# Moving the two half chunks of the last group's output behind its other chunks

## The chip, the cores and the metric

The kernel runs on one core of a Trainium2 chip. Its time is the device time of one execution in microseconds (us), and the figure given is the median of several executions. The core has five engines with an instruction stream each: TensorE (PE in the profile), VectorE (DVE), ScalarE (ACT), GpSimd (POOL) and SyncE (SP), which issues most of the transfers here.

## What is computed

A transformer block with adaptive layer norm over a sequence of 2048 rows of 512 bf16 values: a local dilated attention (32 heads of 16, window 8, stride 2), then a gated feed-forward layer with 1792 hidden columns. The reference, cut to the outer frame and the second half:

```python
def _B_ref(x, w_gate, w_up, w_down):
    g = jnp.einsum('bsd,df->bsf', x, w_gate)
    u = jnp.einsum('bsd,df->bsf', x, w_up)
    h = _gelu(g) * u
    return jnp.einsum('bsf,fd->bsd', h, w_down)
...
h = _layernorm(x, axis=-1) * (1 + ca) + sa
x = x + ga * _A_ref(h, A_wqkv, A_wo)
h = _layernorm(x, axis=-1) * (1 + cb) + sb
x = x + gb * _B_ref(h, B_w_gate, B_w_up, B_w_down)
return x
```

The six vectors `sa` to `gb` come from `silu(c) @ w_mod`. Only the last line and the last product, `h` by `w_down`, are touched by the change, and only for the last 512 of the 2048 rows.

## The kernel before

The rows are split into five groups (`GROUPS`): two of 256 rows and three of 512. Each group passes through a layer norm, the products for q, k and v, the attention, a second layer norm, and the feed-forward layer (`emit_ffn`). The kernel first records all of its work as operations (`Plan.op`), numbered in the order in which they are recorded; each has an engine, an estimated time and a function that issues its instructions. `Plan.order` then puts them into the order of the hand-kept list `ORDER`, and `Plan.emit` issues them in that order. Every engine executes its own instructions in the order in which they were issued, so `ORDER` fixes, for each engine separately, what comes after what. Waits between engines follow from the tiles that are read and written and from the buffers of the tile pools.

`emit_ffn` for one group works in two steps. First, for 14 pieces of 128 hidden columns, 4 matmuls with `Wg` and 4 with `Wu` (line 800) fill two accumulators; ScalarE takes the gelu of the one (line 809) and copies the other (line 811); VectorE multiplies them into the tile `hht` (line 812). Second, the output is made in chunks of 128 rows (`c4`): 14 matmuls over the hidden pieces (line 827) add up the accumulator `y_ps`, VectorE adds the residual row `x` to it and writes `ot` (line 840), and SyncE issues the transfer of `ot` to the output (line 843). The 14 matmuls are recorded as four operations, of 4, 4, 4 and 2 matmuls.

The last group has four such chunks. The last chunk is cut into two halves of 256 of the 512 columns (`parts = 2`), each with its own accumulator, its own 14 matmuls of half the width, its own addition and its own transfer. I call the four chunks **c0**, **c1**, **c2** and the two halves **A** (columns 0 to 255) and **B** (columns 256 to 511). Their operations have the numbers:

| part | matmuls (4, 4, 4, 2) | addition | transfer |
|---|---|---|---|
| c0 | 986, 987, 988, 989 | 990 | 991 |
| c1 | 992, 993, 994, 995 | 996 | 997 |
| c2 | 998, 999, 1000, 1001 | 1002 | 1003 |
| A | 1004, 1005, 1006, 1007 | 1008 | 1009 |
| B | 1010, 1011, 1012, 1013 | 1014 | 1015 |

The accumulators come from a pool with 4 buffers (`psF`), which the gate and up products use as well, and `ot` from a pool with 2. A tile takes its buffer at its first use in `ORDER`, and waits there until the tile that had the buffer before is done. The end of `ORDER` before the change reads

```python
949, 950, 986, 980, 992, 993, 994, 998, 987, 988, 995, 996, 997, 1010, 989, 990, 991, 1011, 999, 1004, 1005, 1012,
1006, 1007, 1013, 1008, 1014, 1015, 1000, 1001, 1009, 1002, 1003,
```

so TensorE ends with the last six matmuls of c2 (1000 and 1001), after both halves; VectorE adds c1, c0, A, B, c2, in this order; and SyncE sends c1, c0, B, A, c2.

Of the kernel before, what the change touches and what calls it, by code (L numbers as in the profile page):

```python
# [15 lines left out]
NEG = -1.0e9  # L16

ORDER = [
    55, 5, 0, 7, 8, 9, 42, 43, 40, 41, 2, 6, 13, 33, 34, 44, 45, 137, 139, 16, 275, 138, 140, 10, 46, 141, 35, 36, 37,
    47, 273, 265, 1, 51, 48, 267, 56, 142, 143, 11, 144, 38, 39, 49, 53, 274, 52, 145, 12, 50, 57, 58, 146, 147, 54,  # L20
    59, 148, 150, 60, 266, 62, 268, 276, 277, 269, 149, 61, 278, 280, 270, 14, 66, 271, 64, 28, 159, 279, 272, 67,
    468, 63, 93, 155, 458, 65, 160, 156, 15, 70, 3, 71, 4, 151, 469, 32, 460, 92, 459, 281, 21, 282, 68, 284, 283, 69,
# [35 lines left out]
    941, 961, 963, 943, 962, 942, 944, 945, 964, 916, 918, 965, 917, 956, 958, 919, 920, 921, 922, 924, 923, 915, 903,  # L58
    971, 957, 959, 960, 973, 967, 966, 968, 969, 981, 925, 982, 983, 972, 974, 951, 970, 975, 984, 953, 927, 926, 928,
    929, 930, 985, 952, 954, 955, 937, 939, 932, 931, 933, 946, 936, 934, 938, 940, 935, 948, 977, 979, 976, 978, 947,  # L60
    949, 950, 986, 980, 992, 993, 994, 998, 987, 988, 995, 996, 997, 1010, 989, 990, 991, 1011, 999, 1004, 1005, 1012,
    1006, 1007, 1013, 1008, 1014, 1015, 1000, 1001, 1009, 1002, 1003,
]


# [149 lines left out]
def kernel(  # L215
# [28 lines left out]
    pl = Plan(tc)  # L244
# [24 lines left out]
    def pri(stage, g, step=0.0):  # L269
        base = {"ln1": PRI_LN1[g], "qkv": PRI_QKV[g], "att": 100 * g, "ln2": 100 * g, "ffn": 100 * g + 1000,  # L270
                "glu": 100 * g - 200}[stage]
        return base + step
# [7 lines left out]
    def h_cols(t, g, dt):  # L280
        n = GROUPS[g][1]
        return t[g][:, dt, 0:n] if len(t[g].shape) == 3 else t[g][:, 0:n // P, dt, :]
# [118 lines left out]
    for b in (1, 0):  # L401
        dma(524e3, lambda dq, b=b: dq.dma_start(
            out=wm01[:, :, b * D:(b + 1) * D], in_=w_mod[:, b * D:(b + 1) * D].rearrange("(t p) n -> p t n", p=P)),
            w=[(wm01, b)], pri=-999.5 + 0.5 * (1 - b), bw=340e3)
# [6 lines left out]
    for d4 in range(4):  # L411
# [3 lines left out]
            pri=-987, bw=200e3)  # L415
# [7 lines left out]
    for i in range(2):  # L423
# [3 lines left out]
            w=[(WdP, ft) for ft in range(lo, hi)], pri=-888 + i, bw=335e3, late=1.0)  # L427
# [359 lines left out]
    def emit_ffn(g):  # L787
        n = GROUPS[g][1]
        nf = SG // n
        hh = []  # L790
        for f0 in range(0, FT, nf):
            p = pri("ffn", g, f0)
            gu = []
            for Wt in (Wg, Wu):
                ps = T("psF", [P, nf, n], F32, "g_ps" if Wt is Wg else "u_ps", "ffn")

                def mm(Wt=Wt, ps=ps, f0=f0):
                    for ft in range(f0, f0 + nf):
                        for dt in range(DT):
                            nc.tensor.matmul(ps[:, ft - f0, :], lhsT=Wt[ft // 7][:, dt, ft % 7 * P:(ft % 7 + 1) * P],  # L800
                                             rhs=h_cols(h2, g, dt), start=(dt == 0), stop=(dt == DT - 1))

                pe(0.866, mm, r=[Wt[f0 // 7], Wt[(f0 + nf - 1) // 7], h2[g]], w=[ps], pri=p)
                gu.append(ps)
            gl = T("gl", [P, nf, n], BF16, "gl")
            ub = T("ub", [P, nf, n], BF16, "ub")
            ht = T("hh", [P, nf, n], BF16, "hht")
            p = pri("glu", g, f0)
            act(0.485, lambda gl=gl, ps=gu[0]: nc.scalar.activation(out=gl[:], in_=ps[:], func=ACT.Gelu_apprx_tanh),  # L809
                r=[gu[0]], w=[gl], pri=p, table="gelu")  # L810
            act(0.475, lambda ub=ub, ps=gu[1]: nc.scalar.copy(out=ub[:], in_=ps[:]), r=[gu[1]], w=[ub], pri=p)  # L811
            dve(0.335, lambda gl=gl, ub=ub, ht=ht: nc.vector.tensor_tensor(out=ht[:], in0=gl[:], in1=ub[:],  # L812
                                                                          op=ALU.mult), r=[gl, ub], w=[ht], pri=p)
            hh.append(ht)
        for c4 in range(n // P):
            gc = GROUPS[g][0] // P + c4
            ot = T("ot", [P, D], BF16, "ot")
            parts = 2 if g == NG - 1 and c4 == n // P - 1 else 1
            w = D // parts
            for part in range(parts):  # L820
                y_ps = T("psF", [P, w], F32, "y_ps", "ffn")
                p = pri("ffn", g, 20 + c4)
                c0 = w * part
                for lo, hi in ((0, 4), (4, 8), (8, 12), (12, 14)):
                    def down(lo=lo, hi=hi, c4=c4, y_ps=y_ps, c0=c0, w=w):
                        for ft in range(lo, hi):
                            nc.tensor.matmul(y_ps[:], lhsT=hh[ft // nf][:, ft % nf, c4 * P:(c4 + 1) * P],  # L827
                                             rhs=WdP[:, ft, c0:c0 + w], start=(ft == 0), stop=(ft == FT - 1))

                    pe(0.2165 / parts * (hi - lo), down, r=hh[lo // nf:hi // nf] + [(WdP, ft) for ft in range(lo, hi)],  # L830
                       w=[y_ps], pri=p)
                p = pri("glu", g, 20 + c4)
                if g < PLAIN:
                    dve(0.6, lambda ot=ot, y_ps=y_ps: nc.vector.tensor_tensor(
                        out=ot[:], in0=y_ps[:], in1=gbB[:], op=ALU.mult), r=[y_ps, gbB], w=[(ot, part)], pri=p)
                    dve(0.335, lambda c4=c4, ot=ot: nc.vector.tensor_tensor(
                        out=ot[:], in0=ot[:], in1=x[g, c4], op=ALU.add), r=[(ot, part), x.key(g, c4)], w=[(ot, part)],
                        pri=p)
                else:
                    dve(0.06 + 0.54 / parts, lambda c4=c4, ot=ot, y_ps=y_ps, c0=c0, w=w: nc.vector.tensor_tensor(  # L840
                        out=ot[:, c0:c0 + w], in0=y_ps[:], in1=x[g, c4][:, c0:c0 + w], op=ALU.add),
                        r=[y_ps, x.key(g, c4)], w=[(ot, part)], pri=p)
                dma(131e3 / parts, lambda dq, gc=gc, ot=ot, c0=c0, w=w: dq.dma_start(
                    out=out[0, gc * P:(gc + 1) * P, c0:c0 + w], in_=ot[:, c0:c0 + w]), r=[(ot, part)], pri=p, late=-0.85)
# [4 lines left out]
    for g in range(NG):  # L849
        ln(g, hT[g], 0, pri("ln1", g), "ln1", LN1_TAGS[g])  # L850
        emit_qkv(g)
        if g == 0:
            mod_row(2, gaB, pri("att", 0, 3.5))
            mod_cols(3, 4, pri("att", 0, 3.6), 8)
            mod_row(5, gbB, pri("att", 0, 3.7))
            dve(1.14, lambda: nc.vector.tensor_tensor(out=woP[:], in0=woP[:], in1=_ap(gaB[:], [[0, 4], [1, D]]),
                                                      op=ALU.mult), r=[woP, gaB], w=[woP], pri=pri("att", 0, 4))
        emit_attention(g)
        if g >= 1:
            emit_ffn(g - 1)  # L860
        if g == PLAIN:
            for f0 in range(0, FT, 2):
                dve(0.6, lambda f0=f0: nc.vector.tensor_tensor(
                    out=WdP[:, f0:f0 + 2, :], in0=WdP[:, f0:f0 + 2, :], in1=_ap(gbB[:], [[0, 2], [1, D]]),
                    op=ALU.mult), r=[(WdP, f0), (WdP, f0 + 1), gbB], w=[(WdP, f0), (WdP, f0 + 1)], pri=500)
    emit_ffn(NG - 1)
    for o in pl.ops:
        if o.dma and o.eng == "sp":
# [30 lines left out]
```

## Time and profile before

| | |
|---|---|
| median of 5 executions | 244.95 us |
| the five | 244.67, 244.72, 244.95, 246.33, 246.73 us |
| the profiled execution | 246.33 us |
| its span, first to last instruction | 244.6 us |
| VectorE, ScalarE, GpSimd busy | 163.5 us (67%), 148.4 us (61%), 25.8 us (11%) |

The profiled execution is one of the five. Its span is 1.73 us shorter than its time, which is what lies before the first and after the last instruction. The last stretch of the span, engine by engine (busy time in us):

| stretch, us | PE | DVE | ACT | POOL |
|---|---|---|---|---|
| 228 to 232 | 3.95 | 0.76 | 0.96 | 0 |
| 232 to 236 | 4.00 | 0.70 | 0 | 0 |
| 236 to 240 | 3.95 | 1.43 | 0 | 0 |
| 240 to 244 | 0.73 | 0.70 | 0 | 0 |

The granted TensorE clock is full (1.000) over the whole span. The second step of the last group's feed-forward layer starts at 228.44 us, and from then on TensorE has nothing else to do.

A row of the timeline gives the start, the duration from the first to the last of a merged run of instructions, the engine, the line, the operation, what it writes and reads, and how many instructions were merged; what the engine waited for before it stands in brackets. A matmul's own duration is longer than the distance from one matmul to the next, since they are pipelined.

### The profile page before, as it was taken

The page shows a single profiled execution, that of the slowest core. Times are in us where ns is not written, and L with a number is a line of the kernel's source. Part 1 is how long each engine was busy: PE and PEld are TensorE (multiplying, and loading weights), DVE is VectorE, ACT ScalarE, POOL GpSimd, SP SyncE. Part 2 cuts the span into 40 slices and gives each one's busy share as a digit, 9 for nine tenths or more (in the row PEclk, how much of TensorE's full clock was granted, in tenths as well). Part 3 has the DMA queues.
Part 4 walks back from the last instruction along what each step waited for, and adds up shares of the span by engine and source line. Part 5 has one row for each costly group of instructions (what it writes and reads, how often), then busy time and mean ns, then how long its engine had stood idle before and what let it go on. Part 6 is the DMA issues. An engine that isn't in the chain of part 4 may idle for free.

```text
span 244.6 us, 4304 instructions
## 1 busy us (share of the span) xinstructions
PE 235.4 (96%) x1660; PEld 128.2 (52%) x1680; DVE 163.5 (67%) x317; ACT 148.4 (61%) x278; POOL 25.8 (11%) x45
## 2 busy tenths in 40 slices
PE   7899999999989999999999999999999999999993
PEld 2499555644459745676444444444444444444461
DVE  4878998999998999679986477983423413221222
ACT  2188799678949663894678956227467541665400
POOL 1287212002000300110000011000001100000000
PEclk9999999999999999999999999999999999999999
DMA  5998999897999438259121914210000412000011
GB/s 173 356 316 247 191 189 243 182 260 173 253 279 253 144 87 178 65 145 146 40 65 25 231 29 89 43 43 1 3 0 0 98 35 86 0 0 0 3 43 43
DMA packets 38970, 29.10 MB, mean 119 GB/s; under 512 B 14117, under 2 KB 38054, under 8 KB 38950
## 3 DMA queue, kind: packets, MB, share of 16 engines
q1 hardware_dynamic: 38800, 28.83, 49.6%
q8 instruction: 13, 0.21, 0.4%
q14 instruction: 7, 0.06, 0.1%
q10 hardware_dynamic: 150, 0.00, 0.0%
HBM read 21.40 MB, written 4.28 MB: 105 GB/s over the span
## 4 chain that ended last, share of the span: by engine, by line
PE 68%; DVE 16%; DMA 9%; issue 2%; POOL 2%; ACT 2%; SPq 0%; DVEq 0%; ACTq 0%; POOLq 0%
PE y_ps L827 20%; PE u_ps L800 19%; PE g_ps L800 18%; PE x_ps L777 4%; DMA Wu<-in_B_w_up_dram 4%; DMA wqkv<-in_A_wqkv_dram 3%; DVE pq L660 3%; DVE pq L654 3%; DVE pv L752 3%; PE o_ps L762 2%; POOL rstd L522 2%; DVE st L516 2%; DVE xn L526 1%; DMA x_sg<-in_A_x_dram 1%; PE LT L670 1%
## 5 line engine op out<-in xcount | busy, mean ns | idle before, releaser
L800 PE MATMUL u_ps<-h2T,Wu 128*128 128x512 bf16 (+1 forms) x280 | 54.4, 336 | 1.4 <-DMA Wu<-in_B_w_up_dram 1.0
L800 PE MATMUL g_ps<-h2T,Wg 128*128 128x512 bf16 (+1 forms) x280 | 54.7, 337 | 0.1
L827 PE MATMUL y_ps<-WdP,hht 128*128 128x512 bf16 (+1 forms) x230 | 49.1, 366 | 0.4
L809 ACT ACTIVATE gl<-g_ps 128x512 bf16<-128x512 f32 x56 | 33.0, 603 | 25.2 <-PE g_ps L800 24.9
L603 PE MATMUL qkv_ps<-hT,wqkv 128*128 128x512 bf16 (+1 forms) x229 | 43.7, 339 | 0.1
L812 DVE TENSOR_TENSOR hht<-gl,ub 128x512 bf16<-128x512 bf16 x56 | 22.6, 421 | 29.8 <-ACT ub L811 21.5
L811 ACT CAST ub<-u_ps 128x512 bf16<-128x512 f32 x56 | 31.7, 589 | 16.0 <-PE u_ps L800 12.8
L800 PEld LDWEIGHTS <-Wu 128*128 128x128 bf16 x280 | 27.0, 98 | 23.8 <-issue 1.5
L800 PEld LDWEIGHTS <-Wg 128*128 128x128 bf16 x280 | 27.0, 98 | 23.0 <-issue 1.5
L827 PEld LDWEIGHTS <-hht 128*128 128x128 bf16 x238 | 23.1, 98 | 24.6 <-issue 0.4
L522 POOL TENSOR_TENSOR rstd<-rstd,neghalf 128x2 f32<-128x2 f32 x16 | 17.5, 1094 | 163.6 <-DVE rstd L511 141.1
L603 PEld LDWEIGHTS <-wqkv 128*128 128x128 bf16 x232 | 24.9, 114 | 13.7 <-issue 1.4
L654 DVE TENSOR_TENSOR pq<-qT,kT 128x2048 bf16<-128x2048 bf16 x24 | 28.8, 1213 | 0.3
L746 DVE TENSOR_TENSOR pv<-e,vR 128x2048 bf16<-128x2048 bf16 x24 | 28.4, 1216 | 0.0
L538 ACT ACTIVATE h2T<-h2T,modT,scl 128x512 bf16<-128x512 bf16 (+1 forms) x20 | 13.2, 727 | 15.0 <-DMA h2T<-xn 15.0
L840 DVE TENSOR_TENSOR ot<-y_ps,x_sg 128x512 bf16<-128x512 f32 (+1 forms) x13 | 8.2, 647 | 18.5 <-PE y_ps L827 18.5
L781 DVE SCALAR_TENSOR_TENSOR x_sg<-x_ps,x_sg 128x512 bf16<-128x512 f32 x16 | 11.0, 686 | 14.2 <-PE x_ps L777 7.2
L777 PE MATMUL x_ps<-woP,oT 128*128 128x512 bf16 x57 | 14.9, 379 | 0.6 <-DVE rinv L723 0.4
L508 ACT ACTIVATE xn<-x_sg,xsum 128x512 bf16<-128x512 bf16 x16 | 11.5, 722 | 4.3 <-DVE xsum L505 4.3
L516 DVE BATCH_NORM_STATS2 st<-x_sg 128x6 f32<-128x512 bf16 x16 | 10.6, 679 | 3.4 <-DMA x_sg<-in_A_x_dram 3.4
L619 ACT CAST kT<-qkv_ps 128x512 bf16<-128x512 f32 x16 | 9.4, 596 | 1.8 <-PE qkv_ps L603 1.8
L619 ACT CAST qT<-qkv_ps 128x512 bf16<-128x512 f32 x16 | 9.5, 598 | 1.3 <-PE qkv_ps L603 1.3
(93 smaller groups left out, 200.9 us busy)
## 6 DMA issues: line engine op xcount, KB each, us to landing
vR<-scr SPq DMA_DIRECT2D x24, 260.0 KB, 5.5
wm<-in_w_mod_dram SPq DMA_DIRECT2D x6, 512.0 KB, 7.0
vR<-scr SPq DMA_DIRECT2D x8, 264.0 KB, 5.2
out_dram<-ot SPq DMA_DIRECT2D x15, 128.0 KB, 1.8
Wg<-in_B_w_gate_dram SPq DMA_DIRECT2D x2, 896.0 KB, 10.7
Wu<-in_B_w_up_dram SPq DMA_DIRECT2D x2, 896.0 KB, 6.3
WdP<-in_B_w_down_dram SPq DMA_DIRECT2D x2, 896.0 KB, 12.9
scr<-vT SPq DMA_DIRECT2D x6, 264.0 KB, 2.8
```

The lines of the kernel that those rows point to most:

```text
L516: dve(0.59, lambda i=i, st=st, c0=c0: nc.vector.bn_stats(out=st[:, i, :], in_=x[g, c0 + i]), r=[x.key(g, c0 + i)], w=[(st, i)], pri=p)
L522: gp(0.65, lambda rstd=rstd: nc.gpsimd.tensor_tensor(out=rstd[:], in0=rstd[:], in1=neghalf[:, 0:2], op=ALU.pow), r=[rstd, neghalf], w=[rst ...
L603: nc.tensor.matmul(ps[:, j - j0, :], lhsT=wqkv[b][:, dt, j:D:4], rhs=h_cols(hT, g, dt), start=(dt == 0), stop=(dt == DT - 1))
L619: act(0.475, lambda t=t, off=off, j0=j0, ps=ps: nc.scalar.copy(out=t[:, j0:j0 + nj, off:off + n], in_=ps[:]), r=[ps], w=[(t, j) for j in r ...
L654: dve(1.14, lambda j=j, wg=wg, t=pq[m]: nc.vector.tensor_tensor(out=t[:], in0=_ap(q[g][:, j, 0:n], [[0, 4], [1, n]]), in1=_ap(k[g][:, j, : ...
L746: dve(1.14, lambda jj=jj, jl=jl, wg=wg, t=pv[m]: nc.vector.tensor_tensor(out=t[:], in0=_ap(e[:, wg, :], [[0, 4], [1, n]]), in1=vR[g][jj][: ...
L777: nc.tensor.matmul(x1_ps[:], lhsT=oT[:, j, c4 * P:(c4 + 1) * P], rhs=woP[:, j, :], start=(j == 0), stop=(j == 3))
L800: nc.tensor.matmul(ps[:, ft - f0, :], lhsT=Wt[ft // 7][:, dt, ft % 7 * P:(ft % 7 + 1) * P], rhs=h_cols(h2, g, dt), start=(dt == 0), stop=( ...
L809: act(0.485, lambda gl=gl, ps=gu[0]: nc.scalar.activation(out=gl[:], in_=ps[:], func=ACT.Gelu_apprx_tanh), r=[gu[0]], w=[gl], pri=p, table ...
L811: act(0.475, lambda ub=ub, ps=gu[1]: nc.scalar.copy(out=ub[:], in_=ps[:]), r=[gu[1]], w=[ub], pri=p)
L812: dve(0.335, lambda gl=gl, ub=ub, ht=ht: nc.vector.tensor_tensor(out=ht[:], in0=gl[:], in1=ub[:], op=ALU.mult), r=[gl, ub], w=[ht], pri=p)
L827: nc.tensor.matmul(y_ps[:], lhsT=hh[ft // nf][:, ft % nf, c4 * P:(c4 + 1) * P], rhs=WdP[:, ft, c0:c0 + w], start=(ft == 0), stop=(ft == FT ...
```

## The change

Three edits. In `emit_ffn` the last operation recorded for each chunk is kept in a list `ends`, and the matmul operations of the two halves name that list as operations that they come after (`after`). The attribute that this sets is read by no code that remains in the kernel: the order comes from `ORDER` alone. The end of `ORDER` is rewritten, and at its start one entry, 44, moves ahead of 33 and 34. Entries 33 and 34 are TensorE's (its first matmuls and the columns of `c`), 44 is VectorE's (an addition of the first layer norm), so no engine's own order changes there.

```diff
-    55, 5, 0, 7, 8, 9, 42, 43, 40, 41, 2, 6, 13, 33, 34, 44, 45, 137, 139, 16, 275, 138, 140, 10, 46, 141, 35, 36, 37,
+    55, 5, 0, 7, 8, 9, 42, 43, 40, 41, 2, 6, 13, 44, 33, 34, 45, 137, 139, 16, 275, 138, 140, 10, 46, 141, 35, 36, 37,
...
-    949, 950, 986, 980, 992, 993, 994, 998, 987, 988, 995, 996, 997, 1010, 989, 990, 991, 1011, 999, 1004, 1005, 1012,
-    1006, 1007, 1013, 1008, 1014, 1015, 1000, 1001, 1009, 1002, 1003,
+    949, 950, 986, 980, 992, 993, 994, 998, 987, 988, 995, 996, 997, 989, 990, 991, 999, 1000, 1001, 1004, 1005, 1006,
+    1007, 1010, 1011, 1012, 1013, 1008, 1014, 1015, 1009, 1002, 1003,
...
-        hh = []
+        hh, ends = [], []
...
-                       w=[y_ps], pri=p)
+                       w=[y_ps], pri=p, after=ends if parts > 1 else ())
+                ends.append(pl.ops[-1])
```

As matmuls on TensorE, the second step of the last group becomes:

| | order (matmuls) |
|---|---|
| before | c0 4, c1 12, c2 4, c0 8, c1 2, B 4, c0 2, B 4, c2 4, A 8, B 4, A 6, B 2, c2 6 |
| after | c0 4, c1 12, c2 4, c0 8, c1 2, c0 2, c2 10, A 14, B 14 |

VectorE's and SyncE's orders stay as they were: the additions c1, c0, A, B, c2 and the transfers c1, c0, B, A, c2.

## The prediction

> **What bounds the kernel now.** I read the page first, for the busy shares and the chain that ended last.
>
> ```profile
> PE 235.4 (96%) x1660; PEld 128.2 (52%) x1680; DVE 163.5 (67%) x317; ACT 148.4 (61%) x278; POOL 25.8 (11%) x45
> ...
> PE 68%; DVE 16%; DMA 9%; issue 2%; POOL 2%; ACT 2%; SPq 0%; DVEq 0%; ACTq 0%; POOLq 0%
> ```
>
> TensorE is busy for 96% of the span and carries 68% of the chain. The change only permutes TensorE work inside the last 17 us, so I then read the chain in order of time at its end (start, duration, what).
>
> ```profile
> 228.88 10.56 PE y_ps L827 x62
> 239.44 0.05 issue
> 239.49 1.26 PE y_ps L827 x5
> 240.74 0.02 issue
> 240.77 0.69 DVE ot L840
> ```
>
> From 228.4 us the chain is output matmuls with no wait for another engine, then one full-width addition. Next the timeline of that stretch, taken in several windows.
>
> ```profile
> 228.44 12.29 PE L827 MATMUL y_ps<-WdP,hht 128*128 128x512 bf16 x68
> 235.12 0.69 DVE L840 TENSOR_TENSOR ot<-y_ps,x_sg 128x512 bf16<-128x512 f32 x1 [5.10 <-PE y_ps L827]
> 235.99 0.69 DVE L840 TENSOR_TENSOR ot<-y_ps,x_sg 128x512 bf16<-128x512 f32 x1 [0.18 <-PE y_ps L827]
> 239.25 0.76 DVE L840 TENSOR_TENSOR ot<-y_ps,x_sg 128x256 bf16<-128x256 f32 x2 [2.57 <-PE y_ps L827]
> 239.60 0.41 DVE L840 TENSOR_TENSOR ot<-y_ps,x_sg 128x256 bf16<-128x256 f32 x1
> 240.77 0.69 DVE L840 TENSOR_TENSOR ot<-y_ps,x_sg 128x512 bf16<-128x512 f32 x1 [0.76 <-PE y_ps L827]
> ...
> 240.04 0.33 SPq L843 DMA_DIRECT2D out_dram<-ot  x1
> 240.42 0.42 SPq L843 DMA_DIRECT2D out_dram<-ot  x1
> 241.48 0.33 SPq L843 DMA_DIRECT2D out_dram<-ot  x1
> ```
>
> The additions are c1, c0, A and B together (the fifth row is B alone), c2. Before each VectorE stands idle until TensorE lets it go: the tail hangs on when each accumulator is complete. The last rows are SyncE's transfers B, A, c2. The DMA view of this stretch closes it:
>
> ```profile
> out_dram<-ot SPq DMA_DIRECT2D x3, 128.0 KB, 1.7
> out_dram<-ot SPq DMA_DIRECT2D x2, 64.0 KB, 1.6
> ```
>
> From issue to landing a full chunk takes 1.7 us and a half 1.6. So the end is: last matmul out at 240.77, c2's addition to 241.46, issue at 241.48, landing near 241.48 + 1.7 = 243.18, and 244.6 - 243.18 = 1.4 us of closing work.
>
> **What the Trainium skill says.** "PSUM — Partial Sum Buffer", section "Engine vs sequencer instructions", has VectorE's queue as strictly first in, first out, and matmuls as completing in program order. The trace agrees as far as it shows: additions start in the listed order, and A and B do not overtake the idle spell of 2.57 us. "TensorE: Matmul & The Clock Gate", "Back-to-back issue gap", gives 518 cycles at 2.4 GHz (216 ns) for a width of 512 and 262 (109 ns) for 256. Here 12 matmuls of 512 span 2.75 us with 379 ns for the last, so (2.75 - 0.379) / 11 = 0.216 us apart; 5 halves span 0.71 with 272 ns for the last, so 0.109: agrees. "DMA: Bandwidth & Descriptors", "Anatomy of one DMA — SWDGE (gpsimd) path", has a fixed part of about 2 us that bytes hardly change. It is stated for another issuing path; the trace's 1.7 against 1.6 us agrees in kind and is what I use.
>
> **The change, part by part.**
>
> *The list `ends`, and entry 44 of `ORDER`: nothing.* No code reads what the first sets. The second changes no engine's own order, so no instruction starts behind another one than before.
>
> *TensorE: 0.* The same 42 full and 28 half matmuls. Before, with a full one last: 41 x 0.216 + 28 x 0.109 + 0.379 = 12.29 us, the shown 12.29. After, with a half last: 42 x 0.216 + 27 x 0.109 + 0.272 = 12.29. The last result is out at the same 240.77. Nothing hides this; it is the same work on the same path. If weight loads (98 ns each) were to show between 28 halves in a row it would cost a few ns each; but 18 to 20 halves stand in a row already, at 109 ns, so I take 0, with 0.1 as the upper bound.
>
> *New waits for buffers: 0.* The five accumulators share four buffers in order of first use, so B, now fifth, takes c0's after c0's addition. B would start at 240.77 - 0.05 - 0.272 - 13 x 0.109 = 239.03; c0's addition started at 235.99 before, and its matmuls now end 0.43 earlier (4 halves of B no longer stand ahead), so it ends by 236.7. Cover: 2.3 us. A takes the buffer of the last up product, whose copy ended at 229.2. A and B's `ot` waits for c1's transfer (issued 235.84, 1.7 us), over before 239.25; c2's for c0's, also early.
>
> *VectorE: later by 0.35.* Here the orders of the two engines part. c2's matmuls are now done at 228.44 + 41 x 0.216 + 0.379 = 237.68. But VectorE's order is still c1, c0, A, B, c2: c2's addition stands behind A's and B's, and B's waits for the last matmul of all. A's is ready 14 halves before the end, 240.77 - 14 x 0.109 = 239.24, as before, and runs to 239.67. Then VectorE is idle with a complete c2 in front of it. At 240.77 B's addition starts; the next follows 0.35 us later (A to B: 239.25 to 239.60), so c2 runs from 241.12 to 241.81, against 241.46.
>
> *SyncE: later by 0.55 in all.* Its order is B, A, c2, and B is the first. A was ready at 239.67 but queues behind B. B ends at 240.77 + 0.41 = 241.18 and is issued at 241.21; A 0.38 later (240.04 to 240.42), at 241.59; it holds the queue 0.42 us, to 242.01, where c2's addition has been over for 0.2 us. c2 goes out at 242.03 instead of 241.48: +0.55. Before, the issues of B and A lay under c2's six matmuls; that cover is gone.
>
> *Landing: 0 to 0.3 more.* Three transfers now go within 0.8 us, 256 KB in place of 128. Before, B and A went 0.38 us apart and neither took above 1.7 us to land, so I take 0. If c2's data had to wait for part of A's it would be up to 0.3; a guess bounded by the landing of A, 241.59 + 1.6 = 243.19, against c2's first bytes some 0.8 us after issue, at 242.83. A gain is excluded, since c2's transfer is no smaller.
>
> Sum: 0 + 0 + 0.55 + 0 = **+0.55 us**, bounds +0.35 (VectorE alone decides) and +0.95 (matmuls 0.1, landing 0.3). Against the profiled execution: span 244.6 to 245.15, time 246.33 to 246.9. That execution was one of the two higher of five; the median is 244.95, so **245.5 us**.
>
> **The rivals.**
>
> *The gain that a half-sized end would bring.* If c2's addition and transfer were done where its matmuls are (237.7), the end would be B alone: 240.77 + 0.41 + 0.03, landing in 1.6, 242.81 against 243.18: -0.4, so 244.55. For it: the idle 2.57 us of VectorE. Against: its order, listed above; nothing moves an addition ahead. This is also the case in which the change would do what its name says for the whole output and not for the matmuls alone. 3%.
>
> *B's matmuls wait for a buffer.* This is slower: if B's buffer came free only with A's addition (239.67, seen by TensorE some 0.04 later), B would start 0.68 after 239.03, and all behind it shift: +0.55 + 0.68 = +1.2, so 246.2. It decides if B's accumulator takes any buffer released after 239.03; by order of first use it is c0's. 4%.
>
> *The landing collides*: up to +0.95, so 245.9. 13%.
>
> *The forecast*: 80%.
>
> **How the numbers follow.** A measurement of this kernel can tell about 1%, 2.4 us, from no change; no case here reaches it. What does move the figure is the spread between executions: three of the five lie at 244.67 to 244.95, two at 246.33 and 246.73, and nothing between. Shifted by 0.55 that is 245.2 to 245.5 and 246.9 to 247.3. If each execution lies high with a chance of 2 in 5, a median of five does with about 0.3, so the range has to reach to 247.0; its lower end, 244.9, takes the bound of +0.35 off the lowest execution (245.0) and a little spread. It leaves out the half-sized end and the highest of the high medians. Within 1%: 0.95; slower by more, a high median with a collision or a buffer wait on top (246.9 + 0.65 = 247.55): 0.04; faster: 0.01.
>
> **What would show it.** Right: 28 half matmuls in one row at the end, the last out near 240.8 (all from 228.44 on), VectorE idle before B's addition for over 1 us, then B and c2 about 0.35 apart; three issues in one run, c2's 0.5 to 0.6 us later after the last matmul than before. Wrong: a full-width addition near 237.8, a gap in the matmuls near 239.0, or a landing of the last transfer well above 1.7 us. Any difference before 228 us would be none of the change's doing by this account.

## The result and the profile after

| | before | after |
|---|---|---|
| median | 244.87 us (80 executions) | 245.57 us (43 executions) |
| lowest | 244.19 us | 245.04 us |
| profiled execution, its span | 246.33, 244.6 us | 245.15, 243.4 us |

The ratio after to before is 1.0034, with a 95% interval of 1.0023 to 1.0045: 0.83 us longer, between 0.56 and 1.10; the two medians lie 0.70 apart. So the change costs a little, within the 1% that counts as no change here.

The span of the profiled execution *after* is shorter by 1.2 us, although the kernel is slower. That comes from ahead of the last stage, which starts 1.90 us earlier. The waits of TensorE in the two traces show where (who waited, for whom, us in total, how often, the longest); first before, then after:

```profile
PE u_ps L800 <- DMA Wu<-in_B_w_up_dram: 1.0, 1, 1.0
PE modT_ps L462 <- DMA wm<-in_w_mod_dram: 0.7, 1, 0.7
```

```profile
PE warm_ps L435 <- DVE neghalf L306: 1.3, 1, 1.3
PE x_ps L777 <- DVE rinv L723: 0.5, 1, 0.5
...
PE modT_ps L462 <- DMA wm<-in_w_mod_dram: 0.2, 1, 0.2
```

In the one execution TensorE waited 1.0 us for a weight transfer near 72 us that in the other was there in time, and 0.5 us more for another: 1.5 of the 1.90. Both lie more than 150 us ahead of the last stage. The only part of the change that lies so early is entry 44, which is tried alone below, and these waits differ between executions of one kernel as well: of three executions of one version below, one waited 1.4 us for `wm`, one 1.0 us for `Wu`, and one for neither. Two single spans therefore say nothing about a change of this size. What can be compared is the **tail**: from the first output matmul of the last group to the end of the span. Before it is 244.6 - 228.44 = 16.16 us. Spans are printed to 0.1 us, so a tail that is worked out from one is good to about 0.05. The timeline after, taken in several windows:

```profile
226.54 12.29 PE L827 MATMUL y_ps<-WdP,hht 128*128 128x512 bf16 x69
...
233.22 1.29 DVE L841 TENSOR_TENSOR ot<-y_ps,x_sg 128x512 bf16<-128x512 f32 x2 [5.10 <-PE y_ps L827]
237.34 0.42 DVE L841 TENSOR_TENSOR ot<-y_ps,x_sg 128x256 bf16<-128x256 f32 x1 [2.83 <-PE y_ps L827]
238.87 1.02 DVE L841 TENSOR_TENSOR ot<-y_ps,x_sg 128x256 bf16<-128x256 f32 x2 [1.10 <-PE y_ps L827]
239.21 0.68 DVE L841 TENSOR_TENSOR ot<-y_ps,x_sg 128x512 bf16<-128x512 f32 x1
...
239.32 0.33 SPq L844 DMA_DIRECT2D out_dram<-ot  x1
239.70 0.42 SPq L844 DMA_DIRECT2D out_dram<-ot  x1
240.22 0.38 SPq L844 DMA_DIRECT2D out_dram<-ot  x1
```

The tail is 243.4 - 226.54 = 16.86 us: **+0.70**. The matmuls take the same 12.29 us. VectorE adds A alone at 237.34, stands idle before it and for 1.10 us after it although c2's accumulator has been complete since about 235.8 (226.54 + 41 x 0.216 + 0.379), then adds B and, 0.34 later, c2 (the fifth row is c2 alone). SyncE sends all three in one run: B, A, c2. Counted from the start of the tail, c2 goes out at 240.22 - 226.54 = 13.68 us, against 241.48 - 228.44 = 13.04 before: 0.64 of the 0.70 is there. The rest is within the rounding of the spans.

The bytes that the DMA engines moved in the changed kernel, from 239 to 242 us in slices of 0.075 us:

```profile
GB/s 0 0 0 0 0 0 0 0 0 0 0 0 0 0 0 96 266 294 185 34 0 55 198 321 226 76 0 14 218 369 341 355 287 151 14 0 0 0 0 0
```

These are B, A and c2, with an empty slice between each and the next: the three transfers move one after the other and don't overlap.

### The profile page after: what moved, and what is told of

It is laid out like the page before. It is cut to its first block, busy times and chain, and to the rows that moved or that the text cites. A ratio compares the mean times of both kernels' runs of the same rounds, so it can differ in the third digit from the quotient of the medians.

```text
span 243.4 us, 4306 instructions
## 1 busy us (share of the span) xinstructions
PE 234.9 (97%) x1661; PEld 128.0 (53%) x1680; DVE 163.3 (67%) x317; ACT 148.4 (61%) x278; POOL 25.8 (11%) x45
## 4 chain that ended last, share of the span: by engine, by line
PE 70%; DVE 17%; DMA 4%; issue 2%; POOL 2%; ACT 2%; DVEq 0%; ACTq 0%; POOLq 0%
PE y_ps L827 20%; PE u_ps L800 20%; PE g_ps L800 19%; PE x_ps L777 4%; DVE pq L654 4%; DVE pq L660 3%; DMA wqkv<-in_A_wqkv_dram 3%; DVE pv L752 3%; PE o_ps L762 2%; POOL rstd L522 2%; DVE st L516 2%; PE LT L670 2%; PE qkv_ps L603 1%; DVE xn L526 1%; DMA x_sg<-in_A_x_dram 1%
```

## The experiments

Each experiment is compared by its tail, read in its own trace, and by its ratio to the kernel before, taken beside it on the same chip. Unless the text says otherwise, an edit is to the end of `ORDER` in the changed kernel, whose last two lines are, from 989 on:

```python
989, 990, 991, 999, 1000, 1001, 1004, 1005, 1006,
1007, 1010, 1011, 1012, 1013, 1008, 1014, 1015, 1009, 1002, 1003,
```

My theory: TensorE loses nothing, and c2's addition and A's and c2's transfers run late because the orders of VectorE and SyncE did not follow that of TensorE. Rival 1: the loss is in TensorE's new order, in buffer waits, or ahead of the last stage. Rival 2: the three late transfers collide.

### c2 done where it is ready

```diff
-989, 990, 991, 999, 1000, 1001, 1004, 1005, 1006,
+989, 990, 991, 999, 1000, 1001, 1002, 1003, 1004, 1005, 1006,
-1007, 1010, 1011, 1012, 1013, 1008, 1014, 1015, 1009, 1002, 1003,
+1007, 1010, 1011, 1012, 1013, 1008, 1014, 1015, 1009,
```

> c2's addition and transfer stand directly behind c2's matmuls; the transfers end B, A as in the changed kernel. Tail means the time from the start of the last group's first output matmul to the end of the span: 16.16 us before, 16.86 us after the change. My theory (the additions and transfers kept their order, so c2's work runs behind B's): SyncE sends B 12.78 us into the tail, A 0.38 later at 13.16, and A's half-sized landing ends it: tail 16.2, so about the time of before, ratio 1.000. Rival 1 (the loss lies in 28 half matmuls in a row, in new buffer waits or ahead of the last stage): the loss stays, ratio 1.003, last matmul later than 12.3 us into the tail. Rival 2 (three transfers in 0.9 us collide on landing): two transfers are left, tail 16.2 or less, landing times of A and B shorter than in the changed kernel.

Measured: tail 245.0 - 228.78 = 16.22, ratio 1.0011 (0.9992 to 1.003). A second time, later:

> The version with c2's addition and transfer early and the transfers B, A at the end, beside it: tail 16.2 us, ratio 1.000; between the two versions A's place in SyncE's queue alone differs, so this one should be 0.5 us slower than the other.

Measured: tail 243.1 - 226.92 = 16.18, ratio 1.002 (1.0004 to 1.0035). The first trace shows c2's addition and c2's transfer, then the transfers of B and A, the last two, in one run:

```profile
238.04 0.69 DVE L841 TENSOR_TENSOR ot<-y_ps,x_sg 128x512 bf16<-128x512 f32 x1 [1.30 <-PE y_ps L827]
...
238.76 0.33 SPq L844 DMA_DIRECT2D out_dram<-ot  x1
241.55 0.81 SPq L844 DMA_DIRECT2D out_dram<-ot  x2
```

TensorE's order is that of the changed kernel, but the tail is back at that of before. Rival 1's part about TensorE's order and its buffers falls. The second ratio lies above what the tail allows: the tail is the same, but the median is 0.24 us higher than that of before beside it. Five of its 22 executions lie above 246 us, against one of 35 of before; whether that is chance or belongs to the kernel is not shown.

### Each chunk sent as soon as it is added

```diff
-989, 990, 991, 999, 1000, 1001, 1004, 1005, 1006,
+989, 990, 991, 999, 1000, 1001, 1002, 1003, 1004, 1005, 1006,
-1007, 1010, 1011, 1012, 1013, 1008, 1014, 1015, 1009, 1002, 1003,
+1007, 1010, 1011, 1012, 1013, 1008, 1009, 1014, 1015,
```

> As c2_early, and A's transfer ahead of B's addition, so that each chunk is sent as soon as it is added. My theory: only B's addition and transfer are left after the last matmul: B is issued 12.78 us into the tail, a half lands 0.1 us faster than a chunk: tail 15.8, 0.36 less than before the change, ratio 0.9985. Rival 1: the loss stays, ratio 1.003. Rival 2: as mine, since nothing is left to collide.

Measured: tail 245.1 - 229.39 = 15.71, ratio 1.0009 (0.998 to 1.0037). Its whole time was left open by the interval, so it ran twice more:

> The version with c2 and A sent when ready, once more, for its time: its tail was 15.7, 0.45 below before, but its 14 executions gave a ratio of 1.0009 with an interval of 0.6%. My theory: tail 15.7 again and ratio 0.998 to 0.9985. Rival (what the tail gains is lost ahead of it): tail 15.7 and ratio 1.000 or more.

> The version with c2 and A sent when ready a third time, because its two intervals (0.998 to 1.0037 and 0.9954 to 1.0007) do not settle whether it is faster than before as a whole. My theory: tail 15.7 us, ratio 0.998 to 0.9985. Rival: tail 15.7 and ratio 1.000 or more.

Measured: tails 243.5 - 227.80 = 15.70 and 242.8 - 227.09 = 15.71; ratios 0.998 (0.9954 to 1.0007) and 0.9996 (0.998 to 1.0011). The timeline of the second of the three, VectorE's last additions (c2, A, B) and SyncE's last transfers (c2, A, B):

```profile
237.07 0.69 DVE L841 TENSOR_TENSOR ot<-y_ps,x_sg 128x512 bf16<-128x512 f32 x1 [1.30 <-PE y_ps L827]
238.60 0.42 DVE L841 TENSOR_TENSOR ot<-y_ps,x_sg 128x256 bf16<-128x256 f32 x1 [0.84 <-PE y_ps L827]
240.12 0.42 DVE L841 TENSOR_TENSOR ot<-y_ps,x_sg 128x256 bf16<-128x256 f32 x1 [1.11 <-PE y_ps L827]
...
237.79 0.33 SPq L844 DMA_DIRECT2D out_dram<-ot  x1
239.05 0.33 SPq L844 DMA_DIRECT2D out_dram<-ot  x1
240.57 0.33 SPq L844 DMA_DIRECT2D out_dram<-ot  x1
```

Nothing but B is left after the last matmul, and the tail is 0.45 us shorter than before the change (0.36 expected), 1.15 shorter than after it. It is the version in which the halves at the end do bring their gain. Whether it is also faster as a whole is not settled: 0.45 us is 0.18%, no wider than the intervals, and the three ratios lie on both sides of 1. Beside the kernel with c2 alone made early, on one chip, its median was 0.58 us lower (244.56 against 245.14), and its tail 0.47: that fits A's place in SyncE's queue, expected as 0.5. The tail shows it; the medians alone, with their upper executions, would not.

### VectorE's or SyncE's order?

The first edit brings c2's addition forward and leaves its transfer last; the second sends A before B and leaves the additions.

```diff
-989, 990, 991, 999, 1000, 1001, 1004, 1005, 1006,
+989, 990, 991, 999, 1000, 1001, 1002, 1004, 1005, 1006,
-1007, 1010, 1011, 1012, 1013, 1008, 1014, 1015, 1009, 1002, 1003,
+1007, 1010, 1011, 1012, 1013, 1008, 1014, 1015, 1009, 1003,
```

> Only c2's addition stands directly behind c2's matmuls; the transfers keep the order B, A, c2. My theory: SyncE's queue sets the end, not VectorE: B waits for the last matmul, A and c2 wait behind B, so c2 goes out at the same 13.6 to 13.7 us into the tail as in the changed kernel: tail 16.8 to 16.9, ratio 1.003. If VectorE's late addition were what costs, the tail would fall by 0.35 or more, to 16.5 or less, ratio 1.0015.

```diff
-1007, 1010, 1011, 1012, 1013, 1008, 1014, 1015, 1009, 1002, 1003,
+1007, 1010, 1011, 1012, 1013, 1008, 1009, 1014, 1015, 1002, 1003,
```

> The additions stay A, B, c2; the transfers become A, B, c2, A's at its addition. My theory: A leaves SyncE's queue 1.5 us before B; B goes out 12.78 us into the tail, c2 as soon as it is added, at 13.38: tail 16.5, 0.3 above before, ratio 1.0014. This would be VectorE's share of the loss by itself. Rival 2 (landing collides): c2's landing from its issue would also fall below that of the changed kernel, by more than 0.1 us.

Measured with c2's addition early: tail 243.7 - 226.82 = 16.88, ratio 1.0026 (1.0006 to 1.0046). The addition now comes more than 3 us sooner, and nothing is won, because SyncE holds B in front:

```profile
236.08 0.69 DVE L841 TENSOR_TENSOR ot<-y_ps,x_sg 128x512 bf16<-128x512 f32 x1 [1.30 <-PE y_ps L827]
...
239.59 0.33 SPq L844 DMA_DIRECT2D out_dram<-ot  x1
239.98 0.90 SPq L844 DMA_DIRECT2D out_dram<-ot  x2
```

c2 was in `ot` at 236.77 and left with the last of these, at 240.45, more than 3 us later.

Measured with A sent first: tail 244.9 - 228.29 = 16.61, 0.1 above the expected 16.5, ratio 1.001 (0.9994 to 1.0026). A, B and c2 go out apart:

```profile
239.54 0.33 SPq L844 DMA_DIRECT2D out_dram<-ot  x1
241.07 0.33 SPq L844 DMA_DIRECT2D out_dram<-ot  x1
241.67 0.33 SPq L844 DMA_DIRECT2D out_dram<-ot  x1
```

c2 leaves 241.67 - 228.29 = 13.38 us into the tail, as expected, 0.34 later than before the change and 0.30 earlier than in the changed kernel. So VectorE's late addition is worth about 0.34 by itself, and SyncE's queue adds about 0.30; but the queue hides the addition entirely, so mending VectorE's order alone wins nothing.

Rival 2 is settled by the landings. From issue to landing, the shortest, the median and the longest: c2 alone in the changed kernel; A and c2 with c2's addition early; B and c2 with A sent first.

```profile
DMA to landing us min/median/max: 1.7/1.7/1.7
...
DMA to landing us min/median/max: 1.6/1.7/1.8
...
DMA to landing us min/median/max: 1.5/1.6/1.7
```

c2, the longest of each, takes 1.7 or 1.8 us behind A and 1.7 with A out of its way. With the bytes of the three apart as well, a collision is worth at most about 0.1 us: rival 2 falls.

### The parts that should do nothing

First the kernel before with only the list of ends and entry 44 moved (the diff against it, a part of the first line of `ORDER`, without the list); then the changed kernel with entry 44 put back, the same edit the other way round; then the changed kernel once more, without an edit.

```diff
-41, 2, 6, 13, 33, 34, 44, 45, 137,
+41, 2, 6, 13, 44, 33, 34, 45, 137,
```

> The kernel before with only the list of ends and entry 44 ahead of 33 and 34; the end of the order is that of before. My theory: neither changes any engine's own order, tail 16.1 to 16.2 us and ratio 1.000 (0.999 to 1.001). Rival (part of the measured 0.3% lies ahead of the last stage, since the tails of the two profiles account for 0.70 of some 0.83 us): ratio 1.001 or more with the tail of before.

> The changed kernel with entries 33, 34, 44 in their order of before. My theory: as the changed kernel, tail 16.8 to 16.9, ratio 1.003. Rival: ratio 1.002 or less with the same tail.

> The changed kernel once more, beside the others on one chip. Tail 16.8 to 16.9 again, ratio 1.003; the start of the last stage may differ by 1 to 3 us between single executions, as it did between all profiles so far (226.5 to 229.4), whatever the kernel.

Measured: list and entry 44 alone, tail 242.9 - 226.76 = 16.14, ratio 0.9984 (0.9965 to 1.0003); the changed kernel without entry 44, tail 244.6 - 227.70 = 16.90, ratio 1.0032 (1.0012 to 1.0051); the changed kernel again, tail 243.4 - 226.51 = 16.89, ratio 1.0043 (1.0021 to 1.0065). With them alone no loss is to be seen, and without entry 44 the loss stays. Rival 1's last place, ahead of the last stage, gets no support from the parts that touch it.

The traces hold the spans in nanoseconds. The last column is the tail from the span so read:

| kernel | start of the tail, us | tail, us | unrounded, us |
|---|---|---|---|
| before | 228.44 | 16.16 | 16.17 |
| list and entry 44 alone | 226.76 | 16.14 | 16.15 |
| changed (twice) | 226.54, 226.51 | 16.86, 16.89 | 16.89, 16.90 |
| changed, without entry 44 | 227.70 | 16.90 | 16.93 |
| c2's addition early | 226.82 | 16.88 | 16.85 |
| A sent first | 228.29 | 16.61 | 16.56 |
| c2 early (twice) | 228.78, 226.92 | 16.22, 16.18 | 16.23, 16.23 |
| all when ready (three times) | 229.39, 227.80, 227.09 | 15.71, 15.70, 15.71 | 15.73, 15.74, 15.73 |

The start moves by 2.9 us over these executions, and by 2.3 within one kernel; the unrounded tails of one kernel agree within 0.01, and those with and without entry 44 within 0.04. Unrounded, the change costs 0.72 in the tail: 0.64 until c2's issue, 0.04 in its landing (1.74 against 1.70 us), and the rest in what follows the landing.

## Why the prediction was right

Forecast +0.55 us and 245.5; measured +0.83 (0.56 to 1.10) and 245.57, of which the tail shows +0.70; the rest, 0.13, is no wider than the interval. That the forecast median is only 0.07 off is in part luck: the sum was 0.15 too small for the tail, but the five executions that it was added to have a median 0.08 above that of the 80.

- **List and entry 44, nothing**: shown by the run that has only these, tail 16.14.
- **TensorE, 0**: the matmuls span 12.29 us in both.
- **Buffer waits, 0**: the matmuls span what the sum without a gap gives. c0's addition followed c1's directly (two in 1.29 us), so B's accumulator was free at 234.51, some 2.6 us ahead of B. The rival that had B waiting for a buffer did not occur.
- **VectorE, +0.35**: c2's addition followed B's by 0.34 us, and with the transfers set right this left c2's issue 0.34 later.
- **SyncE, +0.55 in all**: the right mechanism, undersized. Measured 0.64. B to A was 0.38 as assumed, but from A to c2 it was 0.52, not the 0.44 that I had from A's 0.42 us and a gap of 0.02. The gap was 0.10 (239.70 + 0.42 to 240.22); already between B and A before it had been 0.05 (240.04 + 0.33 to 240.42), which I did not use. It is the one term of the sum that was clearly off.
- **Landing, 0**: between the issue of c2 and the end of the span lie 3.18 us, against 3.12 before; c2's landing stays at 1.7 us, and the bytes of the three transfers don't overlap. The collision did not occur.
- **The half-sized end, -0.4**: not what the change does, as forecast; made true by an edit, it was -0.45.

What failed is beside the sum: the chance of an upper level, which I had from two of five executions. There is an upper group, but it is small: of the 80 executions of before, 73 lie between 244.2 and 245.9, most of them near 244.8, none between 245.9 and 246.3, and 7 above. That is about 1 in 11, not 2 in 5 (after the change 5 of 43 lie above 247, and none between 246.2 and 247.0). The part of the range that rested on it, up to 247.0, was not needed for the median.

## What to carry to other kernels

A chunk is done only when its transfer has landed. In an order written out by hand, moving its matmuls gained nothing here until its addition and its transfer were moved in their own queues as well; the missing moves turned a gain of 0.45 us in the tail into a loss of 0.70. Where several queues follow each other, read which one releases the last transfer: with SyncE holding B in front, an addition 3 us earlier was worth nothing. For an edit near the end of a kernel compare the stretch from the last point that it doesn't touch, since here that repeated to a few hundredths of a microsecond while whole executions differed by some microseconds.

## What the runs showed of the hardware

A transfer that stands directly behind another in SyncE's queue costs more than the 0.33 us that a single issue shows. In the changed kernel the second starts 0.38 us after the first and the third 0.52 us after the second (239.32, 239.70, 240.22), because the second issue itself takes 0.42 us and 0.10 us pass before the third. With c2's addition early, where the third had been ready for more than 3 us, the last step was 0.47 (239.98 to 240.45). So most of the additional time is there without any wait for data; what it is stays open.

Two additions in a row on VectorE start closer together than one takes: two of 128x512 span 1.29 us, where one takes 0.69, so the second starts 0.60 after the first.
